# Turning the scores of the later batches by DMA in two 16-bit parts instead of on the tensor engine

## The chip, the core and the metric

The kernel runs on one core of one Trainium2 chip. The metric is the device time of one execution in microseconds (us); the figure used is the median of several runs. A profiled execution also gives a span, from its first to its last recorded instruction, and a trace of every instruction on every engine: PE (the matrix engine, with its weight loads listed as PEld), DVE (the vector engine), ACT (the scalar engine), POOL and SP. In this kernel POOL and SP only issue DMAs.

## The reference

There are 4 batches of 6080 tokens with 256 channels. Each batch has a channel-by-channel attention, and its output passes through a two-layer network of width 2048.

```python
def _attn_ref(q, k, v, tau):                    # q, k, v: (4, 6080, 256)
    qn = q / (np.linalg.norm(q, axis=1, keepdims=True) + 1e-06)
    kn = k / (np.linalg.norm(k, axis=1, keepdims=True) + 1e-06)
    s = kn.transpose(0, 2, 1) @ qn / tau        # (4, 256, 256): channels x channels
    s = s - s.max(-1, keepdims=True)
    a = np.exp(s)
    a /= a.sum(-1, keepdims=True) + 1e-09
    return (v @ a).astype(np.float32)

def _moe_ref(x, w_in, w_out, s, b):             # x: (24320, 256), w_in: (256, 2048)
    h = x @ w_in
    r = np.maximum(h, 0.0)
    g = s * (r * r) + b
    return (g @ w_out).astype(np.float32)       # w_out: (2048, 256)
```

The scores of a batch need the whole batch: a product of 6080 rows (the Gram matrix) and the two norms of every channel. They are only 256x256 numbers. Because `v @ a @ w_in` equals `v @ (a @ w_in)`, the kernel folds the attention matrix into the input weights once for each batch and never forms the attention output.

## The kernel before

**The main stream.** The 24320 tokens are cut into 48 groups of 512 (the last has 256). A group has 16 steps, numbered `m`; the loop variable is `s = 16 * group + m`. In a step `mm1` multiplies one 128-wide slice of the folded weights `wa` with the group's transposed tokens `vT` into `h_ps` (line 578). After every second step ACT applies the ReLU (`relu`, line 588), and DVE or ACT square it (`square`, lines 601 and 599). The second layer of the group before runs in the same steps on PE, seven matrix instructions to a step (line 746). For all but the first and the last group it is done in seven half-size products (`seven_items`), for which DVE prepares four sums `S` (lines 672 to 678). DVE takes each finished product out of the PSUM bank with one instruction (`evacuate`, line 606): the results named `u` are kept for later, the ones named `o_sb` go to the output. The banks X, Y and Z are reused within a group, so a late `u` holds up the next product that is written into X.

**The side stream.** Everything else is hung onto steps of this loop by `at_step(s, f)`. Instructions keep their program order on each engine (`po`), so an instruction that waits holds up all that stands behind it on its engine. The side stream loads `v` (POOL) and turns it with DMA transposes from SP (`crossbar_v`, line 359, at `m` = 6 two groups ahead). It also prepares the next batch: it loads `q` and `k`, accumulates the Gram matrix in the PSUM bank `s_ps` (line 142), and squares the chunks.

**Norms of a later batch.** Each of its 12 chunks of rows is squared and summed on ACT and DVE into a 128x512 row block `f` (line 178). The blocks of chunks 1 to 11 are then added to that of chunk 0 by an accumulating DMA from POOL (`into_first`, line 188). `add_norms` (line 217) sums the one block that is left over its partitions with four small matrix instructions.

**Finishing a later batch.** `finish_ops` returns a list of small functions, and the table `FIN` says at which step each is issued, counted from 56 steps ahead of the first group that needs the new `wa`. In order: a warming instruction for ACT's square root, `norms` (four matrix instructions and the square root on ACT), `recip` (two tiny DVE operations and one that scales the Gram matrix in PSUM into `sm_s` in SBUF, line 246), a warming instruction for ACT's exponential, `turn` (four fp32 transposes on PE into `t_ps`, line 253), `exps(0)` and `exps(1)` on ACT (line 263), `sums` (row sums on PE and a reciprocal on DVE), and then eight `fold_one` (two matrix instructions on PE each, line 290), scaled out of PSUM by ACT or DVE in turn (lines 283 and 285), three steps apart. All PSUM tiles of this stage come from the one bank that the Gram matrix used.

Batch 0 is finished ahead of the main stream, with the same functions called by hand, and with five matrix instructions of no use (`keep_busy`) between its `recip` and its `turn`.

Of the kernel before, what the change touches and what calls it, by code (L numbers as in the profile page):

```python
# [9 lines left out]
FP16 = mybir.dt.float16  # L10
FP32 = mybir.dt.float32
AF = mybir.ActivationFunctionType
ALU = mybir.AluOpType
# [3 lines left out]
def kernel(  # L17
# [13 lines left out]
    P = 128  # L31
# [22 lines left out]
    def po(ins):  # L54

        tc.keep_in_program_order(ins)
        return ins
# [51 lines left out]
    class Gram:  # L109
# [41 lines left out]
        def norm_ops(self, c):  # L151

            qc, kc = self.tiles[c]
            _, np_, jc = self.chunks[c]
            st = {}

            def squares(a, js):
                def f():
                    if "sq" not in st:
                        st["sq"] = sq_pool.tile([P, 2, JC, C], FP16, tag="sq", name="sq")  # L160
                    if a == 0:
                        po(nc.vector.tensor_mul(
                            st["sq"][:np_, 0, js, :], qc[:np_, js, :], qc[:np_, js, :]))
                    else:
                        po(nc.scalar.activation(  # L165
                            out=st["sq"][:np_, 1, js, :], in_=kc[:np_, js, :], func=AF.Square))
                return f

            def fold(half, arrays, last):
                def f():  # L170
                    src = st["f", 2 * half] if 2 * half < jc else st["sq"]
                    if ("f", half) not in st:
                        if last:
                            t = f3_pool.tile([P, 2, 1, C], FP16, tag="f3", name="f3")
                        else:
                            t = sq_pool.tile([P, 2, half, C], FP16, tag=f"f{half}", name="f")
                        st["f", half] = t
                    po(nc.vector.tensor_add(  # L178
                        st["f", half][:np_, arrays], src[:np_, arrays, :half, :],
                        src[:np_, arrays, half : 2 * half, :]))  # L180
                    if last and (self.b == 0 or c == 0):
                        self.rows.append((st["f", half], np_, 1))
                return f

            def into_first():

                dst, src = self.rows[0][0][:np_], st["f", 1][:np_]
                po(nc.gpsimd.dma_start(out=dst, in_=src, accum_op=ALU.add))  # L188

            def unfolded():  # L190
                self.rows.append((st["sq"], np_, jc))

            ops = []
            for h in range(0, jc, 4):
                js = slice(h, min(h + 4, jc))
                ops += [squares(1, js), squares(0, js)]
            if jc == 2:
                return ops + [unfolded]
            if jc == 8:
                ops += [fold(4, slice(0, 1), False), fold(4, slice(1, 2), False)]  # L200
            ops += [fold(2, slice(0, 2), False), fold(1, slice(0, 2), True)]
            return ops + [into_first] if self.b > 0 and c > 0 else ops

        def add_norms(self, last=False):

# [15 lines left out]
        def finish_ops(self):  # L221
# [9 lines left out]
            def recip():  # L231
                nrm = st["nrm"]
                po(nc.vector.tensor_scalar_add(out=nrm, in0=nrm, scalar1=EPS))
                st["r"] = sm_pool.tile([P, 2, CH], FP32, tag="rnrm", name="rnrm")
                po(nc.vector.reciprocal(out=st["r"], in_=nrm))
                if inv_tau != 1.0:
                    po(nc.vector.tensor_scalar_mul(
                        out=st["r"][:, 0], in0=st["r"][:, 0], scalar1=inv_tau))
                st["s"] = sm_pool.tile([P, CH, C], FP32, tag="sm_s", name="sm_s")
                if self.b == 0:  # L240
                    for ch in range(CH):
                        po(nc.vector.tensor_scalar_mul(
                            out=st["s"][:, ch], in0=self.s_ps[:, ch],
                            scalar1=st["r"][:, 1, ch : ch + 1]))
                else:
                    po(nc.vector.tensor_mul(
                        st["s"], self.s_ps, st["r"][:, 1, :, None].broadcast_to((P, CH, C))))

            def turn():
                st["t"] = self.bank("t_ps", CH, C)  # L250
# [5 lines left out]
            def ready(func):  # L256

                po(nc.scalar.activation(out=warm, in_=ones32[:, 0:1], func=func))

            def exps(j):  # L260
                if j == 0:
                    st["e"] = sm_pool.tile([P, CH, C], FP16, tag="eT", name="eT")
                po(nc.scalar.activation(
                    out=st["e"][:, j, :], in_=st["t"][:, j, :], func=AF.Exp,
                    scale=st["r"][:, 0, j : j + 1]))
                if j == 0:
                    self.wa = apool.tile([P, CH, Dff], FP16, tag="wa16", name="wa16")
# [47 lines left out]
            else:  # L315
                folds = []
            folds += [fold_one(f0, NW, m) for f0 in range(NW if self.b == 0 else 0, Dff, NW)
                      for m in range(CH)]
            return [lambda: ready(AF.Sqrt), norms, recip, lambda: ready(AF.Exp), turn, lambda: exps(0), lambda: exps(1), sums] + folds

        def bank(self, name, a, b):

# [90 lines left out]
    def keep_busy(n, w, x):  # L413

        idle_ps = h_tile("idle_ps")[:, 0, :]
        for _ in range(n):
            po(nc.tensor.matmul(idle_ps, w, x, start=True, stop=True, skip_group_check=True))
# [15 lines left out]
    fin[1]()  # L433
    fin[2]()
    fin[3]()
    keep_busy(5, w_in16[:, 0, :P], w_in16[:, 0, :NW])
    fin[4]()
    transpose_v(0)
    for f in fin[5:12]:
        f()  # L440


# [44 lines left out]
    def at_step(s, f):  # L487
        side.setdefault(int(s), []).append(f)


    FIN = (-12, 0, 3, 3, 6, 8, 10, 13)
    first_group = [b * N // TG for b in range(B)]
    for i, f in enumerate(fin[12:]):
        at_step(i // 2 * 4 - 1 + i % 2 if i > 1 else 0, f)
    at_step(14, lambda: po(nc.vector.tensor_scalar_mul(
        out=s_out, in0=s_bc, scalar1=1.0 / (LAM * LAM))))

# [21 lines left out]
    for b in range(1, B):  # L519
        gr = grams[b]  # L520
        w0 = first_group[b - 1] * FT + (26 if b == 1 else 6)
        w1 = first_group[b] * FT - 3
        NCH = len(gr.chunks)
        fin_len = 54
        span = (w1 - fin_len) - w0 - 12
        n = NCH * JC
        for c in range(NCH):
            sc = w0 + span * c * JC / n
            at_step(max(3, sc - 16), lambda gr=gr, c=c: gr.load(c))
            if c == 0:  # L530
                at_step(sc, gr.start)
            for j in range(JC):
                at_step(w0 + span * (c * JC + j) / n, lambda gr=gr, c=c, j=j: gr.mm(c, j))

            def norm_step(gr=gr, c=c, sc=sc):
                ops = gr.norm_ops(c)
                for i, f in enumerate(ops):
                    at_step(int(sc) + 2 + 1 + i * 3, f)
            at_step(sc + 1, norm_step)

        def fin_step(gr=gr, s=w1 - fin_len):
            ops = gr.finish_ops()
            for i, f in enumerate(ops):
                at_step(int(s) + 1 + (FIN[i] if i < 8 else FIN[7] + 3 + (i - 8) * 3), f)
        at_step(w1 - fin_len - 12, fin_step)


# [222 lines left out]
    for s in range(NS + FT):  # L770
        g, m = divmod(s, FT)
        if g < NG:
            mm1(g, m)

        if m == SHIFT and 0 < g and g - 1 not in plain:
            items = seven_items(g - 1)
            work.append((items, 8 if g == NG - 1 else 7))
        if work:
            items, n = work[0]
            for f in items[:n]:  # L780
                f()
            del items[:n]
            if not items:
                work.pop(0)
        for gp in plain:
            for mp in range(FT):
                if s == gp * FT + PLAG[gp] + (mp * 3 // 2 if gp == 0 else mp):
                    plain_mm2(gp, mp)
        if g < NG and m % 2 == 1:
            relu(g, m // 2)  # L790
            if g in plain:
                late = g > 0 and m // 2 % 2 == 1
                square(g, m // 2, m // 2 + 1, nc.scalar if late else nc.vector)
        if g < NG and g not in plain and m in SQUARES:
            square(g, *SQUARES[m])
        if g == NG - 1 and m in LAST:
            LAST[m]()
        elif m == 0 and 0 < g and g - 1 not in plain:
            square(g - 1, 6, 8, nc.vector)
        elif 0 < g and g - 1 not in plain and m in SUMS:  # L800
            sums_of(g - 1, SUMS[m])
        for f in side.pop(s, []):
            f()
# [34 lines left out]
```

## Time and profile before

| | us |
|---|---|
| median of 4 runs | 723.97 |
| the four runs | 723.69, 723.69, 724.25, 724.56 |
| the profiled execution's own time | 724.56 |
| its span | 722.8 |
| busy in the span: PE / DVE / ACT / POOL | 700.6 / 622.8 / 544.7 / 112.3 |

The profiled execution is the slowest of the four runs; 1.8 us of its time lie outside the span. The tensor engine's granted clock is full in every slice of the span. In the profile, a row of a timeline begins with the start and the length in us, both counted from the start of the span; merged rows carry a count (x4), and a bracket at the end gives the idle time ahead of the row and what ended it.

### The profile page before, as it was taken

The page shows a single profiled execution, that of the slowest core. Times are in us where ns is not written, and L with a number is a line of the kernel's source. Part 1 is how long each engine was busy: PE and PEld are TensorE (multiplying, and loading weights), DVE is VectorE, ACT ScalarE, POOL GpSimd, SP SyncE. Part 2 cuts the span into 40 slices and gives each one's busy share as a digit, 9 for nine tenths or more (in the row PEclk, how much of TensorE's full clock was granted, in tenths as well). Part 3 has the DMA queues.
Part 4 walks back from the last instruction along what each step waited for, and adds up shares of the span by engine and source line. Part 5 has one row for each costly group of instructions (what it writes and reads, how often), then busy time and mean ns, then how long its engine had stood idle before and what let it go on. Part 6 is the DMA issues. An engine that isn't in the chain of part 4 may idle for free.

```text
span 722.8 us, 17624 instructions
## 1 busy us (share of the span) xinstructions
PE 700.6 (97%) x7486; PEld 505.9 (70%) x7486; DVE 622.8 (86%) x871; ACT 544.7 (75%) x589; POOL 112.3 (16%) x191
## 2 busy tenths in 40 slices
PE   4799999999999999999999999999999999999997
PEld 2556777766677777777677777777668777777777
DVE  4779999988889999998788998998888888888886
ACT  4479877887777777788777777778777777777874
POOL 4522331211101222111110222111000000000000
PEclk9999999999999999999999999999999999999999
DMA  9999998556464988465863786835323333321202
GB/s 235 208 259 138 176 159 154 95 110 128 94 117 93 167 144 143 87 107 73 153 129 84 124 145 126 153 82 90 98 67 78 91 72 73 97 59 46 81 30 75
DMA packets 86447, 83.83 MB, mean 116 GB/s; under 512 B 56240, under 2 KB 61504, under 8 KB 86368
## 3 DMA queue, kind: packets, MB, share of 16 engines
q0 software_dynamic: 26176, 43.74, 37.9%
q1 hardware_dynamic: 59616, 37.64, 20.8%
q8 instruction: 59, 0.97, 0.6%
q10 hardware_dynamic: 576, 1.31, 0.5%
q14 instruction: 20, 0.16, 0.1%
HBM read 78.91 MB, written 24.90 MB: 144 GB/s over the span
## 4 chain that ended last, share of the span: by engine, by line
PE 88%; DMA 6%; issue 2%; DVE 1%; ACT 1%; POOL 1%; POOLq 0%; ACTq 0%
PE h_ps L578 43%; PE o_ps L746 38%; PE s_ps L142 4%; PE wa_ps L290 2%; DMA qk<-in_q_dram 2%; DMA w_in<-in_moe_w_in_dram 1%; DMA f<-f 1%; DMA qk<-in_k_dram 1%; ACT r L588 1%; POOL qk L126 1%; PE o_ps L624 1%; PE o_ps L650 0%; DVE S L672 0%; ACT g L599 0%; DVE o_sb L606 0%
## 5 line engine op out<-in xcount | busy, mean ns | idle before, releaser
L588 ACT ACTIVATE r<-h_ps 128x1024 f16<-128x1024 f32 (+1 forms) x384 | 388.0, 1014 | 144.3 <-PE h_ps L578 142.7
L578 PE MATMUL h_ps<-vT,wa 128*128 128x512 f16 (+7 forms) x1632 | 451.8, 364 | 0.6 <-ACT r L588 0.4
L746 PEld LDWEIGHTS <-S 128*128 128x128 f16 x2944 | 197.9, 98 | 85.2 <-DVE S L672 0.4
L746 PEld LDWEIGHTS <-g 128*128 128x128 f16 x2208 | 155.1, 98 | 74.1
L601 DVE TENSOR_TENSOR g<-r 128x2048 f16<-128x2048 f16 (+2 forms) x150 | 174.7, 1164 | 16.5 <-ACT r L588 16.2
L746 PE MATMUL o_ps<-T,S 128*128 128x128 f16 x2208 | 183.2, 219 | 0.3 <-DVE S L672 0.2
L578 PEld LDWEIGHTS <-wa 128*128 128x128 f16 x1632 | 136.2, 98 | 21.2 <-issue 1.0
L746 PE MATMUL o_ps<-w_out,g 128*128 128x128 f16 x1472 | 134.2, 219 | 0.3 <-DVE u L606 0.3
L606 DVE SCALAR_TENSOR_TENSOR o_sb<-o_ps,s_out,u 128x256 f32<-128x256 f32 x138 | 66.4, 481 | 50.2 <-PE o_ps L746 48.1
L599 ACT ACTIVATE g<-r 128x1024 f16<-128x1024 f16 (+1 forms) x97 | 100.4, 1035 | 0.2
L142 PE MATMUL s_ps<-qk 128*128 128x256 f16 (+1 forms) x384 | 69.7, 281 | 14.4 <-ACT qk L133 9.0
L337 POOL DMA_DIRECT2D v<-in_v_dram x48 | 31.9, 672 | 243.9 <-DMA vT<-v 182.2
L188 POOL DMA_DIRECT2D f<-f x33 | 28.9, 877 | 244.5 <-DVE f L178 191.4
L606 DVE SCALAR_TENSOR_TENSOR u<-o_ps,s_out,rowconst 128x256 f32<-128x256 f32 x138 | 65.9, 478 | 1.0 <-PE o_ps L746 1.0
L746 PE MATMUL o_ps<-w_out,S 128*128 128x128 f16 x736 | 63.5, 219 | 0.0
L746 PE MATMUL o_ps<-N,g 128*128 128x128 f16 x736 | 63.4, 219 | 0.0
L165 ACT ACTIVATE sq<-qk 128x1024 f16<-128x1024 f16 (+3 forms) x49 | 50.4, 1033 | 11.6 <-DMA qk<-in_k_dram 6.3
L674 DVE TENSOR_TENSOR S<-S,g 128x2048 f16<-128x2048 f16 (+1 forms) x47 | 56.5, 1201 | 1.3
L672 DVE TENSOR_TENSOR S<-g 128x2048 f16<-128x2048 f16 (+1 forms) x47 | 56.0, 1192 | 0.0
L678 DVE TENSOR_TENSOR S<-g,S 128x2048 f16<-128x2048 f16 x46 | 55.9, 1216 | 0.0
L676 DVE TENSOR_TENSOR S<-g 128x2048 f16<-128x2048 f16 x46 | 55.9, 1214 | 0.0
L142 PEld LDWEIGHTS <-qk 128*128 128x128 f16 (+1 forms) x384 | 32.7, 101 | 20.2 <-DVE qk L132 8.3
(72 smaller groups left out, 322.4 us busy)
## 6 DMA issues: line engine op xcount, KB each, us to landing
out_dram<-o_sb SPq DMA_DIRECT2D x46, 512.0 KB, 3.0
v<-in_v_dram POOLq DMA_DIRECT2D x47, 256.0 KB, 4.8
qk<-in_k_dram POOLq DMA_DIRECT2D x42, 256.0 KB, 6.1
qk<-in_q_dram POOLq DMA_DIRECT2D x42, 256.0 KB, 7.2
f<-f POOLq DMA_DIRECT2D x30, 128.0 KB, 3.0
vT<-v SPq DMA_TRANSPOSE x182, 3.2
w<-in_moe_w_out_dram POOLq DMA_DIRECT2D x4, 512.0 KB, 11.7
raw<-in_q_dram ACTq DMA_DIRECT2D x2, 512.0 KB, 6.9
```

Source lines behind the costliest of these rows:

```text
L142: po(nc.tensor.matmul(self.s_ps[:, ch, :], kc[:np_, j, ts(ch, P)], qc[:np_, j, :], start=(c == 0 and j == 0 and ch == 0), stop=(c == len(s ...
L165: po(nc.scalar.activation(out=st["sq"][:np_, 1, js, :], in_=kc[:np_, js, :], func=AF.Square))
L578: po(nc.tensor.matmul(dst, wa[:, ci, ts(m, P)], src, start=(ci == 0), stop=(ci == CH - 1), skip_group_check=True))
L588: po(nc.scalar.activation(out=r16[:, :, i % 2, :n], in_=h_tiles.pop((g, i))[:, :, :n], func=AF.Relu))
L599: po(nc.scalar.activation(out=dst, in_=src, func=AF.Square))
L601: po(nc.vector.tensor_mul(dst, src, src))
L606: po(nc.vector.scalar_tensor_tensor(out=dst, in0=src, scalar=s_out, op0=ALU.mult, in1=add, op1=ALU.add))
L672: po(nc.vector.tensor_add(T[1], A21, A22))
L674: po(nc.vector.tensor_sub(T[2], T[1], A11))
L676: po(nc.vector.tensor_sub(T[3], A11, A21))
L678: po(nc.vector.tensor_sub(T[4], A12, T[2]))
L746: po(nc.tensor.matmul(st[name][:, j, :], a()[:, i, ts(j, P)], w[:, i, :], start=first, stop=last, skip_group_check=True))
```

## The change

For batches 1 to 3 the scaled Gram matrix is no longer turned on PE. DVE writes it as a 16-bit part `hi` (one instruction) and then the remainder `lo` = scaled value minus `hi`, also in 16 bits (two instructions). Each part is turned by two DMA transposes from SP, and DVE adds the two turned parts into an fp32 tile `t_sb` in SBUF (`join`). The two exponentials read that tile. The list of a later batch has two more entries, and `FIN` is longer: `hi` at 5, `lo` at 7, `join` at 13, the exponentials at 15 and 17, the sums at 20 and the folds from 23 on (they stood at 8, 10, 13 and from 16 on).

There are three smaller edits. The row block of a later batch's last chunk is kept and summed by PE itself, in four more small matrix instructions, and its accumulating DMA goes. In batch 0 there are four instead of five idle matrix instructions, and the entries' numbers shift by one, since the scaling became an entry of its own. In the last group the squares of pairs 0, 2, 4, 6 of steps go to ACT and those of pairs 1, 3, 5, 7 to DVE, where it was the other way round.

```diff
-                    if last and (self.b == 0 or c == 0):
+                    if last and (self.b == 0 or c == 0 or c == len(self.chunks) - 1):
                         self.rows.append((st["f", half], np_, 1))
...
-            return ops + [into_first] if self.b > 0 and c > 0 else ops
+            return ops + [into_first] if self.b > 0 and 0 < c < len(self.chunks) - 1 else ops
...
+            def scale():
                 st["s"] = sm_pool.tile([P, CH, C], FP32, tag="sm_s", name="sm_s")
-                if self.b == 0:
+                for ch in range(CH):
+                    po(nc.vector.tensor_scalar_mul(
+                        out=st["s"][:, ch], in0=self.s_ps[:, ch],
+                        scalar1=st["r"][:, 1, ch : ch + 1]))
+
+            def split(part):
+                st[part] = sm_pool.tile([P, CH, C], FP16, tag=f"s_{part}", name=f"s_{part}")
+                rk = st["r"][:, 1]
+                if part == "hi":
+                    po(nc.vector.tensor_mul(
+                        st["hi"], self.s_ps, rk[:, :, None].broadcast_to((P, CH, C))))
+                else:
                     for ch in range(CH):
-                        po(nc.vector.tensor_scalar_mul(
-                            out=st["s"][:, ch], in0=self.s_ps[:, ch],
-                            scalar1=st["r"][:, 1, ch : ch + 1]))
-                else:
-                    po(nc.vector.tensor_mul(
-                        st["s"], self.s_ps, st["r"][:, 1, :, None].broadcast_to((P, CH, C))))
+                        po(nc.vector.scalar_tensor_tensor(
+                            out=st["lo"][:, ch], in0=self.s_ps[:, ch], scalar=rk[:, ch : ch + 1],
+                            op0=ALU.mult, in1=st["hi"][:, ch], op1=ALU.subtract))
+                st[part + "T"] = sm_pool.tile([P, CH, C], FP16, tag=f"t_{part}", name=f"t_{part}")
+                for ch in range(CH):
+                    po(nc.sync.dma_start_transpose(
+                        out=st[part + "T"][:, :, ts(ch, P)], in_=st[part][:, ch, :]))
+
+            def join():
+                st["t"] = sm_pool.tile([P, CH, C], FP32, tag="sm_s", name="t_sb")
+                po(nc.vector.tensor_add(st["t"], st["hiT"], st["loT"]))
...
+            front = [lambda: ready(AF.Sqrt), norms, recip]
+            if self.b == 0:
+                front += [scale, lambda: ready(AF.Exp), turn]
+            else:
+                front += [lambda: ready(AF.Exp), lambda: split("hi"), lambda: split("lo"), join]
+            return front + [lambda: exps(0), lambda: exps(1), sums] + folds
...
-    keep_busy(5, w_in16[:, 0, :P], w_in16[:, 0, :NW])
     fin[4]()
+    keep_busy(4, w_in16[:, 0, :P], w_in16[:, 0, :NW])
+    fin[5]()
     transpose_v(0)
-    for f in fin[5:12]:
+    for f in fin[6:13]:
         f()
...
-    FIN = (-12, 0, 3, 3, 6, 8, 10, 13)
+    FIN = (-12, 0, 3, 3, 5, 7, 13, 15, 17, 20)
     first_group = [b * N // TG for b in range(B)]
-    for i, f in enumerate(fin[12:]):
-        at_step(i // 2 * 4 - 1 + i % 2 if i > 1 else 0, f)
+    FOLDS = (0, 0, 3, 4, 7, 8)
+    for i, f in enumerate(fin[13:]):
+        at_step(FOLDS[i], f)
...
-                at_step(int(s) + 1 + (FIN[i] if i < 8 else FIN[7] + 3 + (i - 8) * 3), f)
+                at_step(int(s) + 1 + (FIN[i] if i < 10 else FIN[9] + 3 + (i - 10) * 3), f)
...
-                late = g > 0 and m // 2 % 2 == 1
+                late = g > 0 and m // 2 % 2 == 0
                 square(g, m // 2, m // 2 + 1, nc.scalar if late else nc.vector)
```

The list `FOLDS` gives the same steps as the formula that it replaces.

More of the change, by code (lines that the diff above doesn't have):

```diff
@@ L318, in finish_ops @@
                       for m in range(CH)]
-            return [lambda: ready(AF.Sqrt), norms, recip, lambda: ready(AF.Exp), turn, lambda: exps(0), lambda: exps(1), sums] + folds
+            front = [lambda: ready(AF.Sqrt), norms, recip]
[4 more added lines that the diff above has]
+            return front + [lambda: exps(0), lambda: exps(1), sums] + folds
         def bank(self, name, a, b):
```

## The prediction

> **What bounds the kernel now.** I read busy time first, then PE's waits, the chain of waits around the finishing of batch 1 and of batch 2, and last the order on DVE, POOL and SP there. From the page (busy time; share of the chain), PE's waits, and the table by stretches (columns: length, then busy time of PE, PEld, DVE, ACT, POOL):
>
> ```profile
> PE 700.6 (97%) x7486; PEld 505.9 (70%) x7486; DVE 622.8 (86%) x871; ACT 544.7 (75%) x589; POOL 112.3 (16%) x191
> PE 88%; DMA 6%; issue 2%; DVE 1%; ACT 1%; POOL 1%; POOLq 0%; ACTq 0%
> PE o_ps L217 <- DMA f<-f: 1.4, 1, 1.4
> 140.00:185.00 45.00, 43.60 (x466) 30.44 (x463) 38.33 (x54) 35.06 (x42) 6.29 (x12) 1.00 0.56 107
> 317.00:360.00 43.00, 43.00 (x459) 29.98 (x457) 37.17 (x50) 33.51 (x40) 6.65 (x12) 1.00 0.70 117
> 490.00:530.00 40.00, 40.00 (x428) 27.93 (x426) 34.60 (x47) 32.03 (x38) 3.19 (x6) 1.00 0.45 90
> ```
>
> The last three rows are the stretches in which batches 1, 2 and 3 are finished. PE is busy without a gap in two of them, and in the first all but 1.40 us: that is the one wait on `f<-f`. So here an instruction off PE is time off the end, and DVE has room (5 to 7 us in each stretch), as long as nothing it makes for PE comes late. The chain of waits shows what is removed:
>
> ```profile
> 145.00 5.73 DMA f<-f
> 150.73 0.14 issue
> 150.86 0.24 PE o_ps L217 x4
> 156.06 0.44 PE t_ps L253 x4
> ...
> 323.93 0.08 PE o_ps L217 x4
> 328.98 0.44 PE t_ps L253 x4
> ```
>
> The first four are batch 1: the last accumulating DMA lands 5.73 us after its issue, and PE stands for it. The last two are batch 2: no wait, four norm instructions for 0.08 us (0.11 from start to start in the timeline), four transposes for 0.44.
>
> **The change part by part.**
>
> *The fp32 transposes go.* 0.44 us of PE for each of 3 batches: -1.32. A rule of the Trainium skill speaks against this ("VectorE: DVE Perf Modes", "The three transpose paths" and the rules below it): turn 128x128 on TensorE if PSUM will do, since it takes 390 ns there and 1309 ns by DMA. By the rule's figures as durations on one path, the change would cost 4 x (1309 - 390) = 3.7 us a batch, 11 in all; but the rule compares latencies. The trace has pipelined transposes at 0.44 us for four and SP idle between groups, so what counts is whether the DMA's result is late (below), not how long it takes.
>
> *The last chunk's accumulate goes*, four norm instructions come: +0.11 for each batch, +0.33 in all, and -1.40 once. Next late there would be the accumulate of chunk 10, issued at 138.59; with the slowest landing of such a DMA (6.5 us) it is in at 145.1, and PE comes to the norms at 149.46. The last `f` itself is written by 144.71. So the whole 1.40 goes.
>
> *POOL loses these three DMAs*, and what they held up moves forward: the timeline has two `v` loads queued right behind the last accumulate of batch 2.
>
> ```profile
> 308.84 0.85 POOL L188 DMA_DIRECT2D f<-f  x1 [8.74 <-DVE f L178]
> 316.84 0.84 POOL L188 DMA_DIRECT2D f<-f  x1 [7.16 <-DVE f L178]
> 317.48 1.39 POOL L337 DMA_DIRECT2D v<-in_v_dram  x2
> 330.11 0.54 POOL L337 DMA_DIRECT2D v<-in_v_dram  x1 [11.24 <-DMA vT<-v]
> ```
>
> With the accumulate gone the two can go at about 309.5 and 312.5 (when the transposes of 306.28 have landed), clear of the `vT` transposes of 319.98, which then land sooner, and so the `v` load of 330.11 goes some 3 us earlier. No time by itself, but it clears the DMAs for the new transposes.
>
> *DVE's new work.* `hi` replaces `sm_s` (same shape and source, 0.69). New are two `lo` (128x256 from PSUM with a scalar: as L606, 0.48 each, 0.40 from start to start) and `join` (128x512, 16-bit in, fp32 out; between 0.42, the all-16-bit L178 of that size, and 0.69, the fp32 L246; I take 0.69, 0.61 from start to start). That is 1.4 us a batch. DVE's rows at batch 2, with the product that needs the first sum:
>
> ```profile
> 327.31 0.69 DVE L246 TENSOR_TENSOR sm_s<-s_ps,rnrm 128x512 f32<-128x512 f32 x1
> 330.99 0.48 DVE L606 SCALAR_TENSOR_TENSOR o_sb<-o_ps,s_out,u 128x256 f32<-128x256 f32 x1 [1.07 <-PE o_ps L746]
> 333.15 1.22 DVE L672 TENSOR_TENSOR S<-g 128x2048 f16<-128x2048 f16 x1
> 334.74 0.44 PE L746 MATMUL o_ps<-T,S 128*128 128x128 f16 x5
> 337.96 1.23 DVE L601 TENSOR_TENSOR g<-r 128x2048 f16<-128x2048 f16 x1 [0.34 <-ACT r L588]
> 341.40 0.50 PE L746 MATMUL o_ps<-T,S 128*128 128x128 f16 x6
> ```
>
> In the new order `hi` stands two instructions later, so it ends at about 329.5, and both `lo` fit into the 1.07 us ahead of the evacuation at 330.99, less the 0.33 by which PE is now earlier: nearly full, but the first sum is still started by PE's product and stays in time. Price if not: the excess, at most 0.1 a batch. `join` stands ahead of the third sum, two `u` and a square. The last of these `u` frees bank X for the product that starts at 341.40 before. That start comes earlier: by 0.33 (above), 0.08 (row sums now later) and two folds (0.86, moved seven steps on), so 340.13. Counting back 0.48 + 1.14 + 0.39 + 1.13 + 0.61, `join` must start by 336.4; DVE itself comes to it at about 335.5.
>
> *The transposes.* SP issues them one after the other; rows of SP's own, all 182 first, then the four of 319.98:
>
> ```profile
> L359 SPq DMA_TRANSPOSE vT<-v x182: 1167/1244/3352, 49.4 to 682.6; - x182
> DMA to landing us min/median/max: 2.3/3.2/9.1
> ...
> L359 SPq DMA_TRANSPOSE vT<-v x4: 1243/1520/2314, 320.0 to 325.5; - x4
> DMA to landing us min/median/max: 4.1/6.2/7.4
> ```
>
> They are of the same shape. `hi` is there at 329.5; the fourth starts 3 x 1.24 later, 333.3, and lands 2.3 to 3.2 later: 335.6 to 336.5, against the deadline of 336.4. Beside `v` loads (the second pair of rows) it would be 329.5 + 5.5 + 4.1 = 339.1, 2.7 late. I take the first, since the `v` load has moved away, with 0.1 us of stall a batch: +0.3. Behind them on SP stand the group's store and the next four `vT` transposes (333.26 and 333.70 before), about 1.2 us later; `vT` is used 26 steps (21 us) after its issue, so this costs nothing. The exponentials move from `m` = 0, 2 to 7, 9: ACT waits for `join` there, behind the ReLU of `m` = 7 and ahead of that of `m` = 9, which has over 1 us. The folds move by seven steps; the last is 12 steps, some 10 us, ahead of its use: nothing. In the new places the fold at `m` = 5 waits behind ReLU and square on ACT, and the next fold needs its bank three steps later: about 0.5 us in hand.
>
> *Batch 0's idle instruction*: 0.22 us shorter, but PE then stands 0.50 us for `w_in` at 40.65; nothing gained. If that load were early, -0.1 (the transposes wait for the scaling next).
>
> *The tail.* The last square moves from ACT (0.63) to DVE (0.42):
>
> ```profile
> 716.15 0.63 ACT L599 ACTIVATE g<-r 128x512 f16<-128x512 f16 x1
> 716.83 1.86 PEld L624 LDWEIGHTS <-g 128*128 128x128 f16 x18 [0.30 <-ACT g L599]
> ```
>
> It would be ready at 716.57 and not 716.78, about when PE comes to it: -0.2. The other squares only swap; DVE's second sum (a stall of 0.27 at 709.88) keeps one square ahead of it. Bounds: -0.5 to +0.3.
>
> The sum: -1.32 - 1.40 + 0.33 + 0.3 - 0.2 = -2.3, on the profiled execution's own 724.56 (span 722.8, so 720.5). That execution is the slowest of the four; I set the difference against the median: 723.97 - 2.3 = 721.7.
>
> **The rivals.**
>
> *Late join (slower).* The fourth transpose lands as beside `v` loads: 2.7 us late, DVE stands at `join`, bank X comes free late, PE waits. Three times 2.7 in place of 0.3 makes -2.6 + 8.1 = +5.5: 729.5. It eats the gain from 0.87 us late on (landing at 337.3), and is slower by over 0.2% from 1.35 (337.75). For it: landings up to 9.1 us, and a deadline within 1 us of the natural time. Against: the accumulate that queued the `v` loads is gone, and DMA stands idle in parts of these stretches (share 0.45 to 0.70).
>
> *The wait was the profile's.* Landing after 5.73 us, where 3.0 is usual, may be that execution's own; then only 1.3 goes: 722.7, within 0.2%. For it: the profiled run is the slowest. Against: its cause, a `v` load and four transposes issued within 0.7 us of it, is in the program.
>
> *DVE a little late everywhere.* 0.3 to 0.5 us a batch at the first sum or at the folds: 722.6.
>
> The change does what it says: the built program has the three groups of transposes, and no fp32 transpose on PE after batch 0.
>
> **How the numbers follow.** About 1.4 us (0.2%) is what a measurement of this kernel can tell from no change. As forecast, with stalls up to 0.8 in all: 0.62, from 720.9 to 722.4. The wait not there: 0.14. DVE late: 0.10, half of it faster. Late join: 0.14, a fifth of it in the middle. So faster 0.67, same 0.22, slower 0.11. The range leaves out the worst of the late join and a better tail: 720.8 to 724.0.
>
> **What would show it.** Right: no wait of PE on `f<-f`; no L253 after batch 0; in batches 2 and 3 the finishing stretch has PE full and is 0.3 shorter; DVE idle ahead of `join` under 1 us; `v` loads ahead of the `vT` transposes. Wrong: idle time of PE ended by DVE `u` at the start of the third sum's product; DVE idle for over 1 us ahead of `join`; PE standing at the first sum or at `wa_ps`.

## The result, and the profile after

The changed kernel takes 723.03 us (median of 33 runs, 722.60 to 725.05) where the kernel before takes 724.07 in the same comparison (53 runs, 723.25 to 724.63): a ratio of 0.9989, with a 95% interval of 0.9984 to 0.9993. That is 1.04 us faster, where 2.3 was forecast. The profiled execution of the changed kernel took 725.05 (span 723.3) and is the slowest of its 33; the last section shows why, and the medians, not this execution, give what the change is worth.

Busy times and the shares of the chain of waits, from the page of the changed kernel:

```profile
PE 702.2 (97%) x7485; PEld 506.2 (70%) x7485; DVE 626.5 (87%) x880; ACT 544.6 (75%) x589; POOL 109.8 (15%) x188
PE 90%; DMA 5%; DVE 2%; ACT 1%; POOL 1%; issue 0%; DVEq 0%; ACTq 0%; POOLq 0%
```

PE still sets the time. DVE has 3.7 us more work, and its share of the chain goes from 1% to 2%. What PE and DVE waited for (total, times, longest) shows where the gain went:

```profile
PE o_ps L772 <- DVE u L632: 2.4, 2, 2.1
...
DVE t_sb L266 <- DMA t_lo<-s_lo: 2.2, 1, 2.2
```

The wait on `f<-f` is gone, as forecast. In its place stands one wait of 2.1 on a `u` (the other one, of 0.3, was there before the change), and DVE stood once, for 2.2, at `join` (L266) for the transpose of `lo`. Which batch this is shows in the stretches that the prediction read (length, then busy time of PE, PEld, DVE, ACT, POOL, then the granted clock):

```profile
140.00:185.00 45.00, 42.89 (x447) 29.79 (x445) 37.61 (x53) 33.71 (x40) 4.43 (x9) 0.96 0.53 109
317.00:360.00 43.00, 43.00 (x465) 30.18 (x464) 38.78 (x54) 34.47 (x41) 4.76 (x9) 1.00 0.55 105
490.00:530.00 40.00, 40.00 (x433) 27.97 (x431) 36.03 (x51) 32.49 (x38) 2.14 (x4) 1.00 0.39 87
```

It is batch 1 alone; in batches 2 and 3 PE is full. The timeline of batch 1, rows of SP, DVE and PE in order of time:

```profile
157.47 2.48 SPq L261 DMA_TRANSPOSE t_lo<-s_lo  x2
160.63 0.48 DVE L632 SCALAR_TENSOR_TENSOR u<-o_ps,s_out,rowconst 128x256 f32<-128x256 f32 x1
163.34 0.69 DVE L266 TENSOR_TENSOR t_sb<-t_hi,t_lo 128x512 f32<-128x512 f16 x1 [2.23 <-DMA t_lo<-s_lo]
163.95 1.22 DVE L702 TENSOR_TENSOR S<-g 128x2048 f16<-128x2048 f16 x1
165.08 0.48 DVE L632 SCALAR_TENSOR_TENSOR u<-o_ps,s_out,rowconst 128x256 f32<-128x256 f32 x1
...
165.61 0.22 PE L772 MATMUL o_ps<-w_out,g 128*128 128x128 f16 x1 [2.11 <-DVE u L632]
```

DVE was ready for `join` at 161.1. It stood until 163.34, then made the third sum and the `u` of 165.08, and only then could PE write into the bank that this `u` had emptied. The chain of waits puts the length on the transpose (start, length):

```profile
158.76 4.46 DMA t_lo<-s_lo
...
163.95 1.22 DVE S L702
165.16 0.41 DVE u L632
```

4.46 us from issue to landing, where the prediction had reckoned with 2.3 to 3.2. The same rows at batch 2:

```profile
333.88 2.48 SPq L261 DMA_TRANSPOSE t_lo<-s_lo  x2
...
337.58 0.69 DVE L266 TENSOR_TENSOR t_sb<-t_hi,t_lo 128x512 f32<-128x512 f16 x1
```

The second of the two starts at 335.17, and the trace's semaphore records have it landed at 337.46. `join` starts at 337.58 with no wait in its bracket, so the margin here is 0.1.

### The profile page after: what moved, and what is told of

Same layout as the page of the kernel before. It is cut to its first block, busy times and chain, and to the rows that moved or that the text cites. A ratio compares the mean times of both kernels' runs of the same rounds, so it can differ in the third digit from the quotient of the medians.

```text
span 723.3 us, 17651 instructions
## 1 busy us (share of the span) xinstructions
PE 702.2 (97%) x7485; PEld 506.2 (70%) x7485; DVE 626.5 (87%) x880; ACT 544.6 (75%) x589; POOL 109.8 (15%) x188
## 4 chain that ended last, share of the span: by engine, by line
PE 90%; DMA 5%; DVE 2%; ACT 1%; POOL 1%; issue 0%; DVEq 0%; ACTq 0%; POOLq 0%
PE h_ps L604 44%; PE o_ps L772 39%; PE s_ps L142 4%; DMA qk<-in_q_dram 2%; PE wa_ps L309 2%; DMA w_in<-in_moe_w_in_dram 1%; DMA qk<-in_k_dram 1%; ACT r L614 1%; DMA t_lo<-s_lo 1%; POOL qk L126 1%; PE o_ps L650 0%; PE o_ps L676 0%; DVE S L702 0%; ACT g L625 0%; DVE o_sb L632 0%
## 5 line engine op out<-in xcount | busy, mean ns | idle before, releaser
L188 POOL DMA_DIRECT2D f<-f x30 | 26.3, 878 | 224.8 <-DVE f L178 199.1
```

## The experiments

The theory after the result: the forecast gains are there, and one stall of `join` in batch 1 eats some 2 us of them. Its rivals: the stall belongs to the one profiled execution; the wait on `f<-f` was never worth 1.4; the new work slows DVE everywhere. All the times below are medians, and "before" is the kernel before in the same session (724.16, 724.21 and 724.16 in the three sessions).

### The changed kernel once more (after_again)

No edit.

> The changed kernel once more, unaltered. Theory A (a late fourth transpose in batch 1 makes join late, bank X comes free late and PE stands about 2 us): 723.0, and the trace shows one wait of PE on the DVE u, 1.5 to 2.1 us, in batch 1, with t_lo landing over 4 us after its issue. Rival B (the stall is the profiled execution's own, and the rest of the expected gain was never there): 723.0, but this trace shows no such wait, and a span about 2 us shorter than the first trace's.

Measured: 723.12, ratio 0.9985 (0.9978 to 0.9992). Its profile has a span of 721.0 and a full clock throughout. PE's wait on `u` is there again:

```profile
PE o_ps L772 <- DVE u L632: 1.8, 2, 1.5
```

So the stall is the program's own, and it is 1.5 in this execution. It does not need the slow profile of the first run.

### The last chunk's norms alone (norm_only)

```diff
-                    if last and (self.b == 0 or c == 0):
+                    if last and (self.b == 0 or c == 0 or c == len(self.chunks) - 1):
...
-            return ops + [into_first] if self.b > 0 and c > 0 else ops
+            return ops + [into_first] if self.b > 0 and 0 < c < len(self.chunks) - 1 else ops
```

Applied to the kernel before.

> The kernel before with one edit: the last chunk's row block of each later batch is summed by PE and its accumulating DMA goes. Scores are turned on PE as before. My theory: -1.40 for the wait and +0.33 for twelve small matrix instructions, so -1.1 (723.0 beside 724.07). Rival (that wait was the profiled execution's own): +0.3 or no change, 724.1 to 724.4.

Measured: 723.06, ratio 0.9984 (0.9978 to 0.9991), so -1.10, where -1.40 + 0.33 = -1.07 was the sum. In batch 1 the norm instructions now run without a wait:

```profile
149.13 0.34 PE L217 MATMUL o_ps<-ones,f 128*128 128x1 f16 x8
```

This small edit by itself is worth all that the whole change gains. The rest of the change gave, in sum, nothing that can be seen, although its transposes are gone from PE.

### `join` three steps later (late_join)

```diff
-    FIN = (-12, 0, 3, 3, 5, 7, 13, 15, 17, 20)
+    FIN = (-12, 0, 3, 3, 5, 7, 16, 18, 20, 23)
```

Applied to the changed kernel, as are the edits below unless they say otherwise.

> The changed kernel with join three steps later (FIN 16, 18, 20, 23 in place of 13, 15, 17, 20), so that join stands behind the third sum and the square of m = 8 on DVE and some 2.5 us more are allowed for the transposes. Theory A: the stall of batch 1 goes, -1.5 to -2.1 against the changed kernel, 721.0 to 721.5. Rival B: no change, 723.0. Rival C (the extra DVE work itself holds PE up): no change or slower, since the same instructions remain.

Measured: 720.88, ratio 0.9955 (0.9941 to 0.9969), 2.15 less than the changed kernel. The stretch of batch 1 is full:

```profile
140.00:185.00 45.00, 45.00 (x489) 31.59 (x487) 40.23 (x57) 36.03 (x42) 5.30 (x10) 1.00 0.60 111
```

The slow transpose is still slow (the `lo` transposes from issue to landing), but now nobody needs it so soon:

```profile
DMA to landing us min/median/max: 2.3/2.3/4.1
```

ACT, at its exponentials, waits a little in each batch (total, times, longest), and that costs nothing:

```profile
ACT eT L282 <- DVE t_sb L266: 1.9, 3, 0.6
```

### The store behind the transposes (store_later)

On SP the group's output store is issued right behind the fourth transpose. Here, in the groups that finish a batch, it is issued after the next `vT` transposes instead.

```diff
-            store(g, 2 if g == NG - 2 else 0)
+            if g + 5 in first_group[1:]:
+                at_step((g + 2) * FT + 8, lambda: store(g))
+            else:
+                store(g, 2 if g == NG - 2 else 0)
```

> The changed kernel; the output store that stands right behind the two lo transposes on SP is issued behind the next four transposes of v instead (three of 48 stores). If the store's writes hold back the completion of the fourth transpose: it lands 2.3 to 2.6 after its issue in all three batches, and the time falls by 1.5 to 2.1, to 721.0 to 721.5. If the v load or chance holds it back: landing in batch 1 stays above 4 us and the time at 723.0; should the v transposes that now follow at once hold it back, likewise.

Measured: 723.03, ratio 0.9984 (0.9978 to 0.9991), as the changed kernel; the longest landing of a `lo` transpose is 4.1, and PE's longest wait on `u` is 2.0. The store does not slow the transpose.

### `hi` made earlier (early_split)

The trace's packet records gave the next theory. Each of the four transposes ends in 32 completion writes of 4 bytes. In batch 2 all 32 of the last one fall within 0.15 us. In batch 1 thirty fall at 160.60 to 160.75, and the last two at 162.10. In between, one 16 KB packet of queue 8, the instruction queue, is recorded from 161.19 to 162.11. The DMA view of the time from issue to landing of that transpose in batch 1, and of as long a time in batch 2, shows the packet in one and not in the other (packets, MB, share; then the landing):

```profile
q1 hardware_dynamic: 966, 0.70, 51.3%
q8 instruction: 1, 0.02, 1.3%
...
t_lo<-s_lo SPq DMA_TRANSPOSE x1, 4.5
```

```profile
q1 hardware_dynamic: 991, 0.72, 54.7%
...
t_lo<-s_lo SPq DMA_TRANSPOSE x1, 2.3
```

The traces of after_again, late_join and store_later have the same 30 + 2 in batch 1, with the last two at the end of such a packet. So the packet was to be avoided:

```diff
-    FIN = (-12, 0, 3, 3, 5, 7, 13, 15, 17, 20)
+    FIN = (-12, 0, 3, 3, 3, 7, 13, 15, 17, 20)
```

> The changed kernel with `hi` issued in the step of `recip` (entry at 3 in place of 5), so that DVE makes it right behind the reciprocal, about 1.3 us earlier; `lo`, `join` and all else stay. All four transposes are issued about 1.3 us earlier. Theory (in batch 1 the completion of the fourth transpose is held up by one 16 KB instruction packet that takes about 1 us on one of the DMA engines just then): the completion is now clear of that packet, the fourth transpose of batch 1 lands after 2.3 us as in batches 2 and 3, `join` waits for nothing, PE's wait on `u` goes, and the time is that of the changed kernel less the stall of 1.5 to 2.1: 721.2. Rival (the slow landing of 3.9 to 4.5 us belongs to the transposes of this place, whatever the packet): it lands after about 4 us again, at about 161.4, and `join` is 0 to 0.5 us late. Rival (`hi` in the old place of the scaling makes an evacuation late): PE waits on DVE about 150 to 156, and the time is 722 or more.

Measured: 720.91, ratio 0.9955 (0.9942 to 0.9967), with `join` in the place where the change has it. The timeline of batch 1:

```profile
155.87 2.48 SPq L261 DMA_TRANSPOSE t_lo<-s_lo  x2
160.88 0.68 DVE L266 TENSOR_TENSOR t_sb<-t_hi,t_lo 128x512 f32<-128x512 f16 x1
```

And the landings of all its `lo` transposes:

```profile
DMA to landing us min/median/max: 2.3/2.3/2.5
```

The start is 1.6 us earlier than in the changed kernel, all 32 writes of the last transpose fall together at 159.0 to 159.2, no landing of a `lo` is over 2.5, and DVE does not wait. The instruction packet comes at 161.62 and now splits the writes of a later transpose, one that nobody waits for. The rival, that the transposes of this place are slow whatever else goes on, is out. The packet itself was not moved by an experiment, only the transposes. But an ordinary `vT` transpose in after shows the same: it starts at 325.74, thirty of its writes fall at 327.63 to 327.78 and two at 328.72, a packet runs from 327.53 to 328.74, and it lands after 4.1 where the two ahead of it took 2.3 and 2.4.

### The transposes with the accumulate restored (turn_late_acc, turn_only_acc)

In both, the norms of the last chunk are put back as before (the edit of norm_only undone). The first has the `FIN` of late_join, the second that of the change.

> The changed kernel with `join`, exponentials and sums three steps later (as in late_join) and with the accumulating DMA of the last chunk restored: the turning alone, without the stall of `join`, plus the squares of the last group. Theory (the terms of the sum are independent): late_join plus the 1.40 wait less the 0.33 of the norm matmuls, so 720.9 + 1.1 = 722.0, PE again waits 1.4 us on the row block `f`. Rival (the wait on `f` covers for the transposes: norms later by 1.4, everything behind it as well): same time, but then the instruction packet meets other transposes, and the landing of the fourth in batch 1 changes. Rival (the `v` loads behind the accumulate now collide with the new transposes in batches 2 and 3): the fourth lands after 4 us or more there, with no stall left because `join` is late.

Measured: 722.05, ratio 0.9970 (0.9958 to 0.9981). With four norm instructions a batch in both, the time from one batch's norms to the next batch's is a clean measure of what the transposes were worth. Before, in batches 2 and 3:

```profile
323.76 0.24 PE L217 MATMUL o_ps<-ones,f 128*128 128x1 f16 x4
...
496.68 0.24 PE L217 MATMUL o_ps<-ones,f 128*128 128x1 f16 x4
```

and in turn_late_acc:

```profile
323.22 0.24 PE L217 MATMUL o_ps<-ones,f 128*128 128x1 f16 x4
...
495.71 0.24 PE L217 MATMUL o_ps<-ones,f 128*128 128x1 f16 x4
```

172.92 against 172.49: 0.43 a batch, where the prediction took 0.44. (With eight norm instructions and `join` in its early place, in after, it is 172.63: 0.29 less than before, where the prediction took 0.3.) The third theory in the expectation is true in part. A `v` load is issued at 329.46, amid the four transposes of batch 2, and the first of them land late beside it; the landings of all `hi` transposes are

```profile
DMA to landing us min/median/max: 2.6/3.3/4.7
```

with the 4.7 in batch 2. But the last `lo`, which starts at 332.73, still lands after 2.3, in batch 3 as well, and `join` waits for nothing.

> The changed kernel with the accumulating DMA of the last chunk restored, `join` where the change put it. If the landing of the fourth transpose is as in the changed kernel: 723.0 + 1.1 = 724.1, level with the kernel before: the turning alone is worth nothing there, 1.3 saved on PE and 1.5 to 2.1 stood for `join`, less 0.2 in the tail. If the norms, 1.4 later by the wait on `f`, take the transposes past the instruction packet: no stall in batch 1, 722.2. If the accumulate's queue on POOL makes `v` loads late and these meet the transposes in batches 2 and 3, as the prediction had it: a stall of up to 2.7 in each, 726 or more.

Measured: 724.56, ratio 1.0005 (0.9996 to 1.0014). Both waits are in its profile, side by side:

```profile
PE o_ps L772 <- DVE u L632: 1.9, 2, 1.6
PE o_ps L217 <- DMA f<-f: 1.2, 1, 1.2
...
DVE t_sb L266 <- DMA t_lo<-s_lo: 1.7, 1, 1.7
```

The shift of the norms by the wait did not take the transposes past the packet: the packet came later as well (161.75 to 162.68, against 161.19 to 162.11 in the changed kernel). It seems to come at a place in the program, and not at a time. Of the three forecasts the first was nearest; it was 0.5 too low. The turning, with the new squares of the last group, gains nothing with `join` where the change put it; with `join` later it gains 2.2.

### The squares of the last group alone (tail_only)

```diff
-                late = g > 0 and m // 2 % 2 == 1
+                late = g > 0 and m // 2 % 2 == 0
```

Applied to the kernel before.

> The kernel before with the squares of the last group swapped between ACT and DVE, nothing else. As predicted: the last square is 0.2 earlier and PE's last wait on it goes: -0.2, within what can be told from no change. Rival (the swap makes DVE late for the second sum): 0 to +0.3, with a PE wait around 710.

Measured: 724.10, ratio 0.9995 (0.9987 to 1.0004): not to be told from no change, with -0.1 as the middle. The trace shows the step itself, PE's last product with no wait for the square in its bracket:

```profile
716.26 2.46 PE L624 MATMUL o_ps<-w_out,g 128*128 128x256 f16 x21
```

What it is worth can be read in the profiles, free of what differs at the start of a run: from the norms of batch 3 to the end of the span it is 226.11 before (722.79 - 496.68) and 225.88 here, so 0.2 as forecast.

### What exactly `join` holds up (join_behind_sum, join_behind_u)

```diff
-    FIN = (-12, 0, 3, 3, 5, 7, 13, 15, 17, 20)
+    FIN = (-12, 0, 3, 3, 5, 7, 14, 15, 17, 20)    # behind_sum; behind_u has 15 there
```

> The changed kernel with `join` one step later (14 in place of 13), all else in place: on DVE `join` then stands behind the third sum and still ahead of the `u` that PE waits for. In batch 1 the fourth transpose lands at about 163.2 again, about 2 late. Theory (PE waits for that one `u`, and through it for `join`): the sum of 1.13 is now made while DVE would stand for the transpose, so the `u` is late by 2.1 - 1.13 = 1.0 and not by 2.1: PE's wait 1.0 (0.4 to 1.0), and the time 721.9. Rival (PE waits for the sum as well, as the operand of its next product): the same gain, but then the wait named is on S. Rival (the length of the wait has nothing to do with the order on DVE): 723.0 as the changed kernel.

Measured: 721.67, ratio 0.9964 (0.9952 to 0.9977). The wait left is on the `u`, not on the sum:

```profile
162.59 0.69 DVE L266 TENSOR_TENSOR t_sb<-t_hi,t_lo 128x512 f32<-128x512 f16 x1 [0.42 <-DMA t_lo<-s_lo]
163.19 0.48 DVE L632 SCALAR_TENSOR_TENSOR u<-o_ps,s_out,rowconst 128x256 f32<-128x256 f32 x1
...
163.73 0.22 PE L772 MATMUL o_ps<-w_out,g 128*128 128x128 f16 x1 [0.30 <-DVE u L632]
```

In this profile the transpose landed after 3.8, and so the wait is 0.3 and not 1.0; the median has 0.8 over late_join. One step was worth 1.36 of the stall of 2.15.

> The changed kernel with `join` two steps later (15 in place of 13), exponentials and sums where the change put them: `join` stands behind the third sum and behind the `u` as well. Theory (only this `u` carries the lateness of `join` to PE): no wait of PE on `u` above 0.3 in batch 1 though the fourth transpose lands as late as before (3.9 to 4.5 us); ACT waits some 1 to 2 us for `join` at the first exponential; 720.9. Rival (ACT, held at the exponential ahead of a ReLU, makes `h_ps` late): PE waits on ACT r in batch 1, and the time is 721.5 to 723.

Measured: 721.31, ratio 0.9959 (0.9947 to 0.9972). The transpose again landed late (4.2), ACT waited 0.8 for it, and PE did not wait on a `u` in batch 1. The theory holds for the `u`; the time is 0.4 above what it expected. No single wait of PE in its batch 1 accounts for that, and the rival's wait on `r` is not seen there either, so those 0.4 stay open.

### Both margins at once (early_and_late)

`hi` at 3, and `join`, exponentials and sums at 16, 18, 20 and 23.

> The changed kernel with `hi` made early (3 in place of 5) and `join`, exponentials and sums three steps later: the widest margin on both sides, some 3.5 us between landing and use. If nothing is left of the stall after either of the two moves alone, the time is theirs, 720.9. If small stalls of 0.1 to 0.3 a batch were left in either: 720.3 to 720.6.

Measured: 720.72, ratio 0.9953 (0.9940 to 0.9967), the fastest kernel here; its distance of 0.16 to 0.19 to the two moves alone is too small to be told from nothing in five runs each (720.55 to 721.05, against 720.79 to 721.16 and 720.83 to 721.15).

## Why the prediction was right, and where not

The sign and the place of every planned term were right. The size, -1.04 for -2.3, comes from one term that was much too small and from one that was not seen. The second was luck: without the 0.62 at the end of the program, which nobody forecast, the terms below leave -0.4. The -1.04 is itself less than the 1.4 that the prediction took a measurement to tell from no change; it is told from none here because 33 and 53 runs narrow the interval.

| term | forecast | measured | from |
|---|---|---|---|
| fp32 transposes off PE | -1.32 | 3 x -0.43 = -1.29 | turn_late_acc, norms to norms |
| wait on `f<-f`, twelve norm instructions | -1.40 + 0.33 | -1.10 | norm_only |
| squares of the last group | -0.2 | -0.1 | tail_only, in the medians (-0.2 in its profile) |
| end of the program | none | -0.62 | spans, below |
| sum of these | -2.6 | -3.1 | |
| stalls at `join` | +0.3 | +2.1 | after against late_join and early_split |
| in all | -2.3 | -1.0 | after |

Without the stall late_join measures -3.28, so the terms add up to within 0.2. The profiles confirm three of them at once: from the norms of batch 3 to the end it is 226.11 before and 224.86 in turn_late_acc, and the difference of 1.25 is 0.43 (batch 3) + 0.6 (the end) + 0.2 (the squares).

**The step that failed** is "I take the first, since the `v` load has moved away, with 0.1 us of stall a batch". In batches 2 and 3 that step held: landings of 2.3, no wait. In batch 1 the landing is 4.5 in after and 3.9 in after_again, and DVE stood for 2.2 and 1.6. The prediction had this value, 4.1, as the upper end, but only as a landing beside `v` loads, and dropped it when those went. The load was not the reason in batch 1, where the delay ends with the instruction packet. Nor did it hurt in batch 2: the `v` load of 330.11 is at 330.52 in after, in a stretch that lies 1.8 later, so it moved 1.4 earlier and not the 3 forecast, and still stands right ahead of the new transposes. There, and in the two kernels with the accumulate restored (329.46 and 330.97), the `hi` transposes land late (up to 3.6, 4.7 and 4.2), but the last `lo`, which starts 3 to 5 us after the load, lands after 2.3. So the step on POOL guarded against something real that did not reach `join`, and left out what did. The row with the cause was on the page before, `q8 instruction`; the prediction does not reckon with its packets.

**Late join**, the rival on the other side, was right in the path of the lateness, through the `u` and the bank. It was wrong in the cause, `v` loads, and in that it happens in one batch of three; that its 2.7 is near the 2.1 measured is chance. Three times would have given 3 x 2.1 - 3.1 = +3.2.

**The deadline.** 336.4, counted from batch 2 of before, is 161.7 in batch 1 of after (this stretch lies 1.8 later in after, and batch 1 is 176.5 ahead of batch 2). The wait of 2.11 puts it at 163.34 - 2.11 = 161.2. So the prediction had set the deadline half a microsecond too late, which mattered little beside the landing.

**The wait was the profile's** is out: norm_only gained 1.10 in the median of 21 runs. The total could not have told: without the -1.40 the prediction's own terms leave -0.9, so 723.1 and not the 722.7 given for this rival, and that is the time that was measured. **DVE a little late everywhere** is out as well: PE is full in batches 2 and 3, and late_join keeps all the new work and loses nothing.

**The rule that speaks against the change.** The Trainium skill ("VectorE: DVE Perf Modes", "The three transpose paths"), with 390 ns against 1309, would have made +11 of it. (The prediction counted each DMA transpose as one of 128x128, where each turns 128x256; with eight on the DMA's side an estimate from the same figures is +27.) The measurement decides: with enough steps between issue and use the gain is the 0.43 a batch that PE had spent, and the length of the DMA path costs nothing. Where the steps are too few, that length is what one pays.

**Batch 0** shows nothing either way. The first ReLU of the stream is 0.05 to 0.43 earlier than before in the kernels that have this edit, and 0.08 and 0.17 earlier in two that have not.

## What to carry to other kernels

Work can be moved off the engine that sets the time onto a DMA at the full gain, if the consumer stands behind everything with a deadline on its own engine: `join` two or three steps later was worth 1.7 and 2.15, where the whole change gained 1.04. Budget the landing of a DMA by its slowest, not its usual, case, and look in the profile for what else uses the DMA engines at that moment, instruction packets included. And when several edits come as one, measure the smallest by itself: here it is worth as much as all of them together.

## What the runs showed of the hardware that I had not expected

**A data transfer waits for instructions.** One 16 KB packet of the instruction queue held back the last two of a transpose's 32 completion writes. In the eight traces of kernels that issue the transposes in the place of the change or later, the packet takes 0.9 to 1.3 us and the two writes come within 0.02 us of its end. The Trainium skill ("Runtime: NRT & Kernel Launch", "Instruction fetch mechanics") has the refill in 16 KiB blocks and calls its cost mostly hidden. For the engine that fetches that may be so; here the transfer that was under way landed 1.5 to 2.2 us late. In after, 1.35 of it is the delay of the two writes (160.75 to 162.10). Between the last write and the landing another 0.8 goes by in batch 1 that does not in batch 2 (1.1 from 162.11 to 163.22, against 0.3 from 337.16 to 337.46), and that part stays unexplained; the `vT` transpose of 325.74 has it too (1.1, from 328.74 to 329.81).

**A gap of 2.1 us can halve the clock.** In the profiled execution of the changed kernel the stall is followed by this (columns as above, the clock is the number ahead of the last two):

```profile
166.00:168.00 2.00, 2.00 (x19) 1.49 (x17) 2.00 (x3) 0.73 (x1) 0.00 (x0) 0.70 0.16 33
168.00:170.00 2.00, 2.00 (x15) 1.25 (x14) 1.23 (x3) 0.30 (x1) 1.78 (x4) 0.50 0.26 18
170.00:172.00 2.00, 2.00 (x22) 1.31 (x21) 1.16 (x3) 1.02 (x1) 0.86 (x2) 0.95 0.99 177
```

The granted clock is 0.5 for 3.4 us, and the three rows lose 0.6 + 1.0 + 0.1 = 1.7 of full-speed time. Three of the 33 runs (724.65 to 725.05) have a mean clock of 0.997 or 0.998; the other thirty end at 723.59. After gaps of 1.5 and 2.0 in two other profiles the clock stayed full. The Trainium skill ("TensorE: Matmul & The Clock Gate", Part 1) lowers the clock after an idle window of about 3.4; here 2.11 was enough, in some runs.

The trace suggests why only in some. Its clock records change at 16.61, 166.80 and 170.21, after stretches of 150.19 and 3.41, which are 44 and 1 times 3.413; the first full-clock stretches of before, norm_only and late_join (709.97, 706.56 and 703.15) are 208, 207 and 206 times that. On that grid the gap (163.50 to 165.61) lies wholly in the stretch from 163.39 to 166.80, at whose end the clock falls. In store_later the grid cuts the gap of 1.96, so that at most 1.75 of it lies in one stretch; in after_again all 1.52 does. So the place of the gap on the grid seems to count beside its length. No other run with a low clock has a trace, so this is not shown. Without the stall, late_join, early_split and early_and_late spread over 0.5 or less, though in five runs each; and one run of the kernel before (726.15) has a mean clock of 0.998 too, though the one long wait in that kernel's profile is 1.4.

**The end of the program got 0.62 shorter.** From the start of the last DVE instruction to the end of the span it is 3.76 to 3.79 in the three kernels without the DMA turning, and 3.14 to 3.18 in all ten with it. The last DVE rows of before and of after (their spans are 722.8 and 723.3):

```profile
719.01 0.48 DVE L630 SCALAR_TENSOR_TENSOR o_sb<-o_ps,s_out,rowconst 128x256 f32<-128x256 f32 x1 [1.26 <-PE o_ps L624]
```

```profile
720.12 0.48 DVE L656 SCALAR_TENSOR_TENSOR o_sb<-o_ps,s_out,rowconst 128x256 f32<-128x256 f32 x1 [1.26 <-PE o_ps L650]
```

The trace's records of SP show what differs. Before, SP takes up five semaphores in turn from the landing of the last store on (2.26, 2.34, 2.41, 2.79 and 2.88 after that start), and with the turning it takes up one (2.26), since the others come ahead of it. That this order is what makes the difference was not varied by itself.
